# Soft-MoE attention: six of eight batches taken two at a time in logits, dispatch softmax and slot products

## The chip, the cores and the metric

The kernel runs on one core of a Trainium2 chip. The metric is the device time of one execution in microseconds (us), lower is better: the median of three runs before the change is 376.43 us (376.32 to 376.77). Of one further execution there is a profile with a trace of every instruction.

## What is computed

First attention for 8 batches, 12 heads, 448 tokens and head size 64, with a sigmoid in place of a softmax. Its result, 3584 tokens of 768 numbers, goes through a soft mixture of 8 experts with 4 slots each (32 slots):

```python
scores = scale * np.matmul(q, k.transpose(0, 1, 3, 2)) - np.log(S)
attn = 1.0 / (1.0 + np.exp(-scores))
x = np.matmul(attn, v)                # then (8 * 448, 768)
...
logits = x @ phi                      # (3584, 32)
d = np.exp(logits - logits.max(0, keepdims=True))
d /= d.sum(0, keepdims=True) + 1e-09  # dispatch: over all tokens
slot_input = d.T @ x
...
h = np.maximum(slot_input[e] @ w1[e], 0.0)
slot_out[e] = h @ w2[e]
...
c = np.exp(logits - logits.max(1, keepdims=True))
c /= c.sum(1, keepdims=True) + 1e-09  # combine: over the slots
out = c @ slot_out
```

All data are float32. The weights w1 and w2 are 50 MB together, q, k and v 33 MB, the output 11 MB.

## The kernel before, in words

Two heads are a head pair, six pairs a batch, 48 in all. Attention goes through a list `seq` of 168 steps, 21 for a batch. At step i TensorE computes the scores of `seq[i]` (`score`, L205) for a block of 128 keys, ScalarE makes the sigmoid (L213), and TensorE multiplies the block of step i - 2 with v (`weigh`, L246): scores run `LAG` = 2 steps ahead. When a head pair is done, ScalarE copies one half of its result out of PSUM (`evac_a`, L249) and VectorE adds the other (`evac_b`, L253). The result is x, with the 128 rows of a head pair as partitions and 448 tokens as columns: tile x0 holds head pairs 0 to 2, xy pairs 3 to 5 of the batch at hand.

Dispatch softmax and slot inputs are made batch by batch while attention goes on, with a maximum that is carried from batch to batch. Four blocks of 128 tokens (`NBK`) hold a batch, the last half filled. The functions are:

- `turns` (L271): VectorE transposes x in 32 x 32 blocks into y (tokens as partitions; y0 for head pairs 0 to 2, y1, which lies in the tile wpe, for 3 to 5). Each of its three calls a batch puts 16 transposes into the queue `todo`; `work` hands them out step by step, by estimated costs and a table `rate`.
- `logits_job` (L287, L295): 24 matmuls of phi and x. For a float32 matmul the trace has two rows. Phi's 32 slots are the columns of the stationary operand, so four matmuls lie side by side in the array, one for each group of 32 columns (j = 0 to 3): group j takes 32 of every 128 tokens. Groups 0 and 1 get 128 moving columns, groups 2 and 3 get 96.
- `softmax_a`, `softmax_b`, `softmax_c` (L304 to L334): maxima, subtraction, sigmoids on ScalarE, reciprocal, product, transposes and sums on VectorE. The logits stay in `lt` for the combine.
- `slot_job` (L340, L359): 32 matmuls, for 4 token blocks, 2 halves of the head pairs and 4 groups of columns; then one VectorE instruction adds the rescaled old sum.

For batch b with u = 21 (b + 1) + 2, the logits come ahead of step u + 1, the sigmoids in u + 2, `softmax_c` in u + 3 and the slot job at the end of step u + 9 (`SLOT_AT`); `slot_job` first hands out all that is left in `todo`. The last batch has a function of its own (`last_job`). The instructions of an engine run in the order in which the code issues them; an engine that waits holds all that stands behind it.

All weight loads go through SP's queue, in units of 384 KB. 56 units (`N_A`) are loaded during attention, spread over the first 140 steps (`W_STEPS`), into the tiles wa0 to wa13, two into wpe near its end, 12 into space that attention leaves, and the rest in transfers of 1536 KB whenever tiles of the ring come free. Behind attention follow the matmuls with w1 (L126), the combine softmax and its transposes (L575), the matmuls with w2 (L645) and the output (L596, L597).

The functions that the change touches:

Of the kernel before, what the change touches and what calls it, by code (L numbers as in the profile page):

```python
# [23 lines left out]
W_STEPS = 140  # L24
# [29 lines left out]
def soft_moe_attention(ctx: ExitStack, tc: tile.TileContext, qk, v, vl, phi, w, wq, wz, cst, out):  # L54
# [13 lines left out]
    lts = [cpool.tile([P, B // 2, P], F32, name=f"lt{t}") for t in range(2)]  # L68
# [4 lines left out]
    def lt_of(b):  # L73
        return lts[b // 4][:, b % 4, :]
# [56 lines left out]
    with ExitStack() as actx:  # L131
# [133 lines left out]
        def turns(t, k0, n):  # L265
            y = (y0, y1)[t]

            def one(a, g):
# [2 lines left out]
                nc.vector.transpose(  # L271
                    y[32 * g:32 * g + 32, k0:k0 + n, 0:nblk(g), BLK * a:BLK * a + BLK], src)
# [19 lines left out]
        def logits_job(b):  # L292
            lg = ps_sc.tile([P, 2, 512], F32, name="sc")[:, 0, :]
            logits(lg, b, range(NPR))
            nc.vector.tensor_copy(lt_of(b)[0:64, :], lg[0:64, 0:P])  # L295
            nc.vector.tensor_copy(lt_of(b)[64:128, 0:96], lg[64:128, 0:96])
            softmax_a(b)

        def softmax_a(b):
            t1 = small.tile([P, 2, 132], F32, name="t1")  # L300
            zt, ls = t1[:, 0, :], lt_of(b)
            for j in range(4):
                r = slice(32 * j, 32 * j + 32)
                nc.vector.tensor_reduce(out=m1[0:32, j:j + 1], in_=ls[r, 0:BLK * nblk(j)], axis=AX.X, op=ALU.max)  # L304
            if b:
                nc.vector.tensor_copy(m1[0:32, 4:5], mz[0:32, (b - 1) % 2:(b - 1) % 2 + 1])
            nc.vector.tensor_reduce(out=m1[0:32, 5:6], in_=m1[0:32, 0:5 if b else 4], axis=AX.X, op=ALU.max)
            new, old = mz[:, b % 2:b % 2 + 1], mz[:, (b - 1) % 2:(b - 1) % 2 + 1]
            for j in range(4):
                nc.vector.tensor_copy(new[32 * j:32 * j + 32, :], m1[0:32, 5:6])  # L310
            if b:
                nc.vector.tensor_tensor(out=zt[:, P:P + 1], in0=old, in1=new, op=ALU.subtract)
            nc.vector.tensor_scalar(zt[:, 0:P], ls, new, None, op0=ALU.subtract)
            dts[b] = t1

        def softmax_b(b):
            zt, pe = dts[b][:, 0, :], dts[b][:, 1, :]
            n = P if b == 0 else P + 1
            nc.scalar.activation(pe[:, 0:n], zt[:, 0:n], AF.Sigmoid)
            nc.scalar.activation(zt[:, 0:n], zt[:, 0:n], AF.Sigmoid, scale=-1.0)  # L320

        def softmax_c(b):
            zt, pe = dts[b][:, 0, :], dts[b][:, 1, :]
            n = P if b == 0 else P + 1
            nc.vector.reciprocal(zt[:, 0:n], zt[:, 0:n])
            nc.vector.tensor_tensor(out=pe[:, 0:n], in0=pe[:, 0:n], in1=zt[:, 0:n], op=ALU.mult)
            nc.vector.transpose(zt[:, 0:P], pe[:, 0:P])
            if b == 0:
                nc.vector.tensor_reduce(out=mz[:, 2:3], in_=pe[:, 0:P], axis=AX.X, op=ALU.add)
            else:  # L330
                nc.vector.tensor_reduce(out=zb, in_=pe[:, 0:P], axis=AX.X, op=ALU.add)
                nc.vector.scalar_tensor_tensor(
                    out=mz[:, 2:3], in0=mz[:, 2:3], scalar=pe[:, P:P + 1], in1=zb, op0=ALU.mult, op1=ALU.add)
            nc.vector.transpose(lt_of(b), lt_of(b))  # L334

        def slot_mm(sls, zt, b, ts, cs=range(NBK), stop=True):
            for c in cs:
                for t in ts:
                    for a in range(4):
                        nc.tensor.matmul(  # L340
                            sls[t][32 * a:32 * a + 32, :], zt[:, c * BLK:(c + 1) * BLK],
                            y_of(t, b)[:, :, c, BLK * a:BLK * a + BLK], start=(c == 0), stop=stop and c == NBK - 1)
# [102 lines left out]
        for b in range(B):  # L445
            u = b * per_b + LAG
            late[u + 10] = [lambda: turns(0, 0, 3)]
            if b < B - 1:
                late[u + 17] = [lambda: turns(1, 0, 2)]
                late[u + 20] = [lambda: turns(1, 2, 1)]  # L450
        for b in range(B - 1):
            u = (b + 1) * per_b + LAG
# [4 lines left out]
            rate.update({u - 2: 1, u - 1: 1, u: 0, u + 1: 0, u + 2: 1.2, u + 3: 0.6, u + 4: 1.2})
# [10 lines left out]
        for i in range(len(seq) + LAG):  # L468
            for f in early.get(i, ()):
                f()  # L470
            if i < len(seq):
# [80 lines left out]
    def combine_softmax(b):  # L552
        lt = lt_of(b).rearrange("p (j s) -> p j s", j=NBK)
        nc.vector.tensor_reduce(out=cm, in_=lt, axis=AX.X, op=ALU.max)
        nc.vector.tensor_tensor(out=lt, in0=lt, in1=cm.unsqueeze(2).broadcast_to([P, NBK, NSLOT]), op=ALU.subtract)  # L555
# [3 lines left out]
        nc.vector.reciprocal(cz, cz)
        nc.vector.tensor_tensor(out=lt, in0=lt, in1=cz.unsqueeze(2).broadcast_to([P, NBK, NSLOT]), op=ALU.mult)  # L560

    def combine_split(b):
        lt = lt_of(b).rearrange("p (j s) -> p j s", j=NBK)
# [4 lines left out]
        return c4

    def combine_turn(b, c4):  # L570
        pt = ps_t.tile([P, 512], F32, name="pt")
        for c in range(NBK):
            n = P if c < 3 else 64
            c0 = c * P if b % 2 == 0 else (c * P + 64) % 448
            nc.tensor.transpose(  # L575
                out=pt[:, c0:c0 + n], in_=c4[0:n, c].rearrange("p a z s -> p (a z s)").bitcast(F32),
                identity=csb[0:n, 0:n])
        at0 = S * b
        while at0 < S * (b + 1):
# [140 lines left out]
```

## Time and profile before

| what | before |
|---|---|
| median of three runs | 376.43 us |
| span of the profiled execution, first to last instruction | 375.5 us |
| TensorE busy | 354.5 us (94%) |
| VectorE busy | 252.7 us (67%) |
| ScalarE busy | 223.9 us (60%) |
| read and written in HBM | 83.59 and 11.01 MB |

In the rows of a profile PE is TensorE, PEld its weight load, DVE VectorE, ACT ScalarE, POOL GpSimd and SP the engine that issues the DMAs; L340 is line 340 of the kernel. A row of the timeline gives start, duration, engine, line, operation, written and read tile, shape and count of a merged group. A row of the groups gives, behind the bar, busy time, mean ns of one, and idle time before them. A row of a windows table gives the stretch, then for PE, PEld, DVE, ACT and POOL the busy time and the number of instructions, then TensorE's granted clock, the DMA share and GB/s. An engine's busy time says nothing of whether others wait for it; that is read where two engines meet.

### The profile page before, as it was taken

The page shows a single profiled execution, that of the slowest core. Times are in us where ns is not written, and L with a number is a line of the kernel's source. Part 1 is how long each engine was busy: PE and PEld are TensorE (multiplying, and loading weights), DVE is VectorE, ACT ScalarE, POOL GpSimd, SP SyncE. Part 2 cuts the span into 40 slices and gives each one's busy share as a digit, 9 for nine tenths or more (in the row PEclk, how much of TensorE's full clock was granted, in tenths as well). Part 3 has the DMA queues.
Part 4 walks back from the last instruction along what each step waited for, and adds up shares of the span by engine and source line. Part 5 has one row for each costly group of instructions (what it writes and reads, how often), then busy time and mean ns, then how long its engine had stood idle before and what let it go on. Part 6 is the DMA issues. An engine that isn't in the chain of part 4 may idle for free.

```text
span 375.5 us, 10520 instructions
## 1 busy us (share of the span) xinstructions
PE 354.5 (94%) x4374; PEld 160.3 (43%) x4374; DVE 252.7 (67%) x681; ACT 223.9 (60%) x309; POOL 5.5 (1%) x25
## 2 busy tenths in 40 slices
PE   8999999999999999999999999999999996999750
PEld 4333444344444444344444444444456552433530
DVE  0048877885979588869869795889655873223560
ACT  4777676766768676767667676768673122423550
POOL 1000000000000000000000000000000000100000
PEclk9999999999999999999999999999999998999895
DMA  7778575766667675766675765534569999999998
GB/s 234 240 233 263 184 234 184 245 210 229 194 200 224 225 223 181 236 227 215 205 225 180 249 227 177 176 101 125 162 186 370 410 426 425 424 427 404 375 404 291
DMA packets 34927, 95.28 MB, mean 254 GB/s; under 512 B 3648, under 2 KB 17344, under 8 KB 33088
## 3 DMA queue, kind: packets, MB, share of 16 engines
q1 hardware_dynamic: 34880, 94.62, 72.3%
q8 instruction: 34, 0.56, 0.6%
q14 instruction: 13, 0.11, 0.1%
HBM read 83.59 MB, written 11.01 MB: 252 GB/s over the span
## 4 chain that ended last, share of the span: by engine, by line
PE 81%; DMA 8%; DVE 6%; ACT 1%; issue 1%; ACTq 0%; DVEq 0%
PE sc L205 34%; PE av L246 33%; DMA wpe<-in_wz_dram 8%; PE sc L287 3%; PE sc L340 3%; PE av L596 2%; PE av L645 1%; PE pt L596 1%; DVE tmp L546 1%; DVE tmp L545 1%; PE av L221 1%; ACT lt L556 1%; PE av L436 1%; DVE lt L555 1%; DVE sm L557 1%
## 5 line engine op out<-in xcount | busy, mean ns | idle before, releaser
L213 ACT ACTIVATE att<-sc,sm 128x896 f32<-128x896 f32 x167 | 168.3, 1008 | 85.1 <-PE sc L205 82.2
L205 PE MATMUL sc<-qk 64*64 64x448 f32 x1336 | 157.5, 543 | 0.0
L246 PE MATMUL av<-att,v 64*64 64x448 f32 x1128 | 131.2, 536 | 0.0
L205 PEld LDWEIGHTS sc<-qk 64*64 64x64 f32 x1336 | 49.7, 134 | 71.0 <-issue 58.4
L271 DVE STREAM_TRANSPOSE wpe<-xy 32x256 f32<-32x256 f32 (+3 forms) x224 | 76.9, 343 | 3.7
L246 PEld LDWEIGHTS av<-att,v 64*64 64x64 f32 x1128 | 42.8, 133 | 63.4 <-issue 61.6
L271 DVE STREAM_TRANSPOSE y<-x 32x288 f32<-32x288 f32 (+1 forms) x128 | 66.5, 520 | 2.0
L253 DVE TENSOR_TENSOR x<-x,av 128x448 f32<-128x448 f32 x24 | 14.9, 621 | 31.6 <-PE av L246 24.6
L246 PE MATMUL av<-att,vl 64*64 64x448 f32 x188 | 22.3, 536 | 0.0
L253 DVE TENSOR_TENSOR xy<-xy,av 128x448 f32<-128x448 f32 x23 | 14.3, 621 | 9.8 <-ACT xy L249 4.4
L126 PE MATMUL av<-wa,jt 128*32 128x256 f32 x336 | 18.5, 380 | 0.1
L126 PEld LDWEIGHTS av<-wa,jt 128*32 128x32 f32 x336 | 10.7, 110 | 7.2 <-DVE jt L402 0.2
L597 ACT COPY wa<-av 128x384 f32<-128x384 f32 x22 | 10.5, 480 | 5.3 <-PE av L596 4.9
L596 PE MATMUL av<-lt,wb 128*128 128x384 f32 x28 | 13.0, 464 | 0.5 <-DVE lt L631 0.5
L597 DVE COPY wa<-pt 128x384 f32<-128x384 f32 x22 | 11.4, 556 | 2.5 <-PE pt L596 2.3
L249 ACT COPY x<-av 128x448 f32<-128x448 f32 x24 | 12.5, 522 | 0.0
L249 ACT COPY xy<-av 128x448 f32<-128x448 f32 x23 | 12.1, 524 | 0.0
L246 PEld LDWEIGHTS av<-att,vl 64*64 64x64 f32 x188 | 7.3, 133 | 10.8 <-issue 10.8
L645 PE MATMUL av<-wa,jt 128*32 128x384 f32 x112 | 11.7, 517 | 0.0
L359 DVE SCALAR_TENSOR_TENSOR jt<-jt,t,sc 128x192 f32<-128x192 f32 x6 | 2.5, 413 | 13.6 <-PE sc L340 13.6
L645 PE MATMUL av<-wa,hw 128*32 128x384 f32 x112 | 11.5, 511 | 0.1
L596 PE MATMUL pt<-lt,wb 128*128 128x384 f32 x28 | 10.5, 374 | 1.1 <-DVE lt L631 1.1
(131 smaller groups left out, 223.1 us busy)
## 6 DMA issues: line engine op xcount, KB each, us to landing
wa<-in_w_dram SPq DMA_DIRECT2D x56, 384.0 KB, 4.0
wa<-in_wq_dram SPq DMA_DIRECT2D x14, 1536.0 KB, 22.6
qk<-in_qk_dram SPq DMA_DIRECT2D x47, 448.0 KB, 3.7
v<-in_v_dram SPq DMA_DIRECT2D x48, 192.0 KB, 2.6
out_dram<-wa SPq DMA_DIRECT2D x12, 384.0 KB, 6.8
out_dram<-wa SPq DMA_DIRECT2D x5, 768.0 KB, 6.2
wb<-in_w_dram SPq DMA_DIRECT2D x6, 384.0 KB, 4.3
wb<-in_w_dram SPq DMA_DIRECT2D x3, 768.0 KB, 7.5
```

The lines of the kernel that those rows point to most:

```text
L126: nc.tensor.matmul(ph[32 * j:32 * j + 32, 0:256], phi_sb[:, kc, :], utile[("w1", e, j, kc // 3)][:, kc % 3 * 256:(kc % 3 + 1) * 256], star ...
L205: nc.tensor.matmul(sc[h][64 * t:64 * t + 64, 0:S], qkts[pt][r, S + k0:S + k0 + 64], qkts[pt][r, 0:S], start=True, stop=True)
L213: nc.scalar.activation(att[:], tile2[:, :, 0:S], AF.Sigmoid, bias=nbias, scale=QSCALE)
L246: nc.tensor.matmul(o[t][r, 0:S], w, att[row, h, :], start=start, stop=stop)
L249: nc.scalar.copy(x_of(p), avs[p][1][:, 0:S])
L253: nc.vector.tensor_tensor(out=x_of(p), in0=x_of(p), in1=av[0][:, 0:S], op=ALU.add)
L271: nc.vector.transpose(y[32 * g:32 * g + 32, k0:k0 + n, 0:nblk(g), BLK * a:BLK * a + BLK], src)
L287: nc.tensor.matmul(lg[32 * j:32 * j + 32, BLK * c0:BLK * n], phi_sb[:, hp, :], blocks(x_of(b * NPR + hp)[:, c0 * P:], j, n - c0), start=(h ...
L340: nc.tensor.matmul(sls[t][32 * a:32 * a + 32, :], zt[:, c * BLK:(c + 1) * BLK], y_of(t, b)[:, :, c, BLK * a:BLK * a + BLK], start=(c == 0) ...
L596: nc.tensor.matmul(pf[:, 0:HALF], ct_of(m, step), sts[hf], start=True, stop=True)
L597: (nc.scalar.copy, nc.vector.tensor_copy)[n % 2](ov, pf[:, 0:HALF])
L645: nc.tensor.matmul(po[32 * fl:32 * fl + 32, 0:HALF], h[:, k:k + NSLOT], ut, start=(n == 0), stop=(n == 2 * E - 1))
```

## The change

Batches (0, 1), (2, 3) and (4, 5) become pairs, batches 6 and 7 stay single (`GROUPS`). Two batches have 896 tokens, exactly seven blocks of 128 (`NB2`). For a pair there is one logits job, one softmax over 224 columns and one slot job over seven blocks, at the places where the second batch of the pair had its own; the first batch of a pair has none. Since x of the first batch must last until the pair's logits, it lies in two weight tiles' space (`wx`, the tiles wa12 and wa13), as do three further blocks of y for each half (`ye`) and the pair's softmax tile (`t1e`). The eight units of those tiles are loaded behind the third pair; the other 48 are spread over 130 steps. A second batch's tokens start in the middle of block 3, so its transposes go to shifted places, 24 a call in place of 16. The host no longer turns the queries of odd batches round by 64 tokens, and the combine takes a pair as pieces of four and three blocks. The core of the diff:

```diff
-W_STEPS = 140
+W_STEPS = 130
+N_X = 8
+GROUPS = ((0, 1), (2, 3), (4, 5), (6,), (7,))
+NB2 = 2 * NBK - 1
...
+        wx = [wpa.tile([P, 4 * UNIT], F32, name=f"wa{(N_A - N_X) // 4 + n}") for n in range(N_X // 4)]
+        xe = [wx[0][:, t * TR * S:(t + 1) * TR * S].rearrange("p (k s) -> p k s", k=TR) for t in range(2)]
...
-        for y in (y0, y1):
-            nc.gpsimd.memset(y[64:128, :, NBK - 1, :], 0.0)
...
-            for g in range(4):
+            if b % 2 == 0 or b >= B - 2:
+                moves = [(g, g, nblk(g), y) for g in range(4)]
+            else:
+                moves = [(g, g + 2, NBK - 1, ye[t]) for g in range(4)]
+                moves += [(g, g - 2, 1, y[:, :, NBK - 1:NBK, :]) for g in (2, 3)]
+            for mv in moves:
                 for a in range(4):
-                    todo.append((0.0335 * n * nblk(g) + 0.18, lambda a=a, g=g: one(a, g)))
+                    todo.append((0.0335 * n * mv[2] + 0.18, lambda a=a, mv=mv: one(a, *mv)))
...
+                for hp in range(NPR):
+                    xa, xb = x_of(g[0] * NPR + hp), x_of(g[1] * NPR + hp)
+                    for x, c0 in ((xa, (0, 0, 0, 0)), (xb, (4, 4, 3, 3))):
+                        for j in (3, 2, 1, 0):
+                            n = nblk(j) if x is xa else NB2 - c0[j]
+                            nc.tensor.matmul(
+                                lg[32 * j:32 * j + 32, BLK * c0[j]:BLK * (c0[j] + n)], phi_sb[:, hp, :],
+                                blocks(x, j if x is xa else (j + 2) % 4, n),
+                                start=(hp == 0 and x is xa), stop=(hp == NPR - 1 and x is xb))
+                nc.vector.tensor_copy(lt, lg[:, 0:NB2 * NSLOT])
...
-            slot_mm([sl[:, t, :] for t in range(2)], dts[b][:, 0, 0:P], b, (0, 1))
+            slot_mm([sl[:, t, :] for t in range(2)], dts[gi][:, 0, :], gi, (0, 1), range(w // NSLOT))
...
-        for b in range(B - 1):
-            u = (b + 1) * per_b + LAG
+        for gi in range(len(GROUPS) - 1):
+            u = (GROUPS[gi][-1] + 1) * per_b + LAG
...
-            rate.update({u - 2: 1, u - 1: 1, u: 0, u + 1: 0, u + 2: 1.2, u + 3: 0.6, u + 4: 1.2})
+            rate.update({u - 2: 1, u - 1: 1, u: 0, u + 1: 0, u + 2: 1.0, u + 3: 0.4, u + 4: 1.2})
...
-                while state["next"] < min(N_A, (i + 1) * N_A // W_STEPS):
+                while state["next"] < min(N_A - N_X, (i + 1) * (N_A - N_X) // W_STEPS):
+                    load(1)
+                if i > W_STEPS and i % 2 == 1 and state["next"] < N_A:
                     load(1)
```

What this does to the order on VectorE, between the softmax of batch 1 (before) and its slot result: the rows start with the addition that makes x of the next batch's first head pair; t and lt are softmax tiles, xy is x of pairs 3 to 5, wpe their y, and the last row takes the slot result.

```order
L253 TENSOR_TENSOR x_91<-x_91,av_878 128x448
L325 RECIPROCAL t_911<-t_911 128x129
L326 TENSOR_TENSOR t_911<-t_911 128x129
L327 STREAM_TRANSPOSE t_911<-t_911 128x128
L331 TENSOR_REDUCE sm<-t_911 128x1
L332 SCALAR_TENSOR_TENSOR sm<-sm,t_911 128x1
L334 STREAM_TRANSPOSE lt_68<-lt_68 128x128
L271 STREAM_TRANSPOSE wpe<-xy 32x4x32 x8
L271 STREAM_TRANSPOSE wpe<-xy 32x3x32 x3
L253 TENSOR_TENSOR x_91<-x_91,av_965 128x448
L271 STREAM_TRANSPOSE wpe<-xy 32x3x32 x5
L359 SCALAR_TENSOR_TENSOR jt<-jt,t_911,sc 128x192
```

The same place with the change, for batches 2 and 3; wa_85 holds the pair's softmax and the further blocks of y.

```order
L359 RECIPROCAL wa_85<-wa_85 128x225
L360 TENSOR_TENSOR wa_85<-wa_85 128x225
L361 STREAM_TRANSPOSE wa_85<-wa_85 128x224
L365 TENSOR_REDUCE sm<-wa_85 128x1
L366 SCALAR_TENSOR_TENSOR sm<-sm,wa_85 128x1
L368 STREAM_TRANSPOSE lt_68<-lt_68 128x224
L285 STREAM_TRANSPOSE wpe<-xy 32x2x32 x7
L285 STREAM_TRANSPOSE wa_85<-xy 32x3x32 x5
L267 TENSOR_TENSOR wa_84<-wa_84,av_1744 128x448
L285 STREAM_TRANSPOSE wa_85<-xy 32x3x32 x11
L285 STREAM_TRANSPOSE wpe<-xy 32x32 x8
L394 SCALAR_TENSOR_TENSOR jt<-jt,wa_85,sc 128x192
```

Behind the addition for the second head pair stood five transposes, now nineteen; the last eight are the first 64 tokens of the second batch, which go into block 3 of wpe.

On TensorE the slot job before, two rows for each token block (y is y0, wpe is y1):

```order
L340 MATMUL sc<-y_94,t_911 32x96 x4
L340 MATMUL sc<-wpe,t_911 32x96 x4
L340 MATMUL sc<-y_94,t_911 32x96 x4
L340 MATMUL sc<-wpe,t_911 32x96 x4
L340 MATMUL sc<-y_94,t_911 32x96 x4
L340 MATMUL sc<-wpe,t_911 32x96 x4
L340 MATMUL sc<-y_94,t_911 32x96 x4
L340 MATMUL sc<-wpe,t_911 32x96 x4
```

And with the change; wa_85 in the last row holds blocks 4 to 6:

```order
L374 MATMUL sc<-y_96,wa_85 32x96 x4
L374 MATMUL sc<-wpe,wa_85 32x96 x4
L374 MATMUL sc<-y_96,wa_85 32x96 x4
L374 MATMUL sc<-wpe,wa_85 32x96 x4
L374 MATMUL sc<-y_96,wa_85 32x96 x4
L374 MATMUL sc<-wpe,wa_85 32x96 x4
L374 MATMUL sc<-y_96,wa_85 32x96 x4
L374 MATMUL sc<-wpe,wa_85 32x96 x4
L374 MATMUL sc<-wa_85 32x96 x24
```

The eight groups of a batch are followed by six more for the three further blocks; the eighth row, block 3 of wpe, is the one that the eight transposes named above complete.

More of the change, by code (lines that the diff above doesn't have):

```diff
@@ L67, in soft_moe_attention @@
     mz, cm, cz, m1, cw = sm[:, 5:9], sm[:, 9:13], sm[:, 13:17], sm[:, 17:23], sm[:, 24:32]
-    lts = [cpool.tile([P, B // 2, P], F32, name=f"lt{t}") for t in range(2)]
+    lts = [cpool.tile([P, B // 2 * P], F32, name=f"lt{t}") for t in range(2)]
     jt = small.tile([P, 2 * SLN], F32, name="jt")
@@ L71, in soft_moe_attention @@
     phi_sb = jt[:, SLN:2 * SLN].rearrange("p (k s) -> p k s", k=NKC)
-    def lt_of(b):
-        return lts[b // 4][:, b % 4, :]
+    lt_at, ltw = [], [0, 0]
+    for gi, g in enumerate(GROUPS):
+        i, wd = gi // 2 - gi // 4, (NB2 if len(g) == 2 else NBK) * NSLOT
+        lt_at.append(lts[i][:, ltw[i]:ltw[i] + wd])
+        ltw[i] += wd
     nc.vector.memset(acc, 0.0)
@@ L290, in logits, with logits_job @@
                         start=(hp == 0), stop=(hp == NPR - 1 and c1 == NBK))
-        def logits_job(b):
+        def logits_job(gi):
+            g, lt = GROUPS[gi], lt_at[gi]
             lg = ps_sc.tile([P, 2, 512], F32, name="sc")[:, 0, :]
[L294 to L301, printed above, removed]
+            if len(g) == 1:
+                logits(lg, g[0], range(NPR))
+                nc.vector.tensor_copy(lt[0:64, :], lg[0:64, 0:P])
+                nc.vector.tensor_copy(lt[64:128, 0:96], lg[64:128, 0:96])
+            else:
+                for hp in range(NPR):
[8 more added lines that the diff above has]
+                nc.vector.tensor_copy(lt, lg[:, 0:NB2 * NSLOT])
+            softmax_a(gi)
@@ L302, in softmax_a @@
+        def softmax_a(gi):
+            t1 = t1e if len(GROUPS[gi]) == 2 else small.tile([P, 2, 132], F32, name="t1")
+            zt, ls = t1[:, 0, :], lt_at[gi]
+            w = ls.shape[1]
             for j in range(4):
                 r = slice(32 * j, 32 * j + 32)
-                nc.vector.tensor_reduce(out=m1[0:32, j:j + 1], in_=ls[r, 0:BLK * nblk(j)], axis=AX.X, op=ALU.max)
-            if b:
-                nc.vector.tensor_copy(m1[0:32, 4:5], mz[0:32, (b - 1) % 2:(b - 1) % 2 + 1])
@@ L307, in softmax_a @@
-            nc.vector.tensor_reduce(out=m1[0:32, 5:6], in_=m1[0:32, 0:5 if b else 4], axis=AX.X, op=ALU.max)
-            new, old = mz[:, b % 2:b % 2 + 1], mz[:, (b - 1) % 2:(b - 1) % 2 + 1]
+                n = w if len(GROUPS[gi]) == 2 else BLK * nblk(j)
+                nc.vector.tensor_reduce(out=m1[0:32, j:j + 1], in_=ls[r, 0:n], axis=AX.X, op=ALU.max)
+            if gi:
+                nc.vector.tensor_copy(m1[0:32, 4:5], mz[0:32, (gi - 1) % 2:(gi - 1) % 2 + 1])
+            nc.vector.tensor_reduce(out=m1[0:32, 5:6], in_=m1[0:32, 0:5 if gi else 4], axis=AX.X, op=ALU.max)
@@ L309, in softmax_a @@
+            new, old = mz[:, gi % 2:gi % 2 + 1], mz[:, (gi - 1) % 2:(gi - 1) % 2 + 1]
             for j in range(4):
                 nc.vector.tensor_copy(new[32 * j:32 * j + 32, :], m1[0:32, 5:6])
[L311 to L318, printed above, removed]
+            if gi:
+                nc.vector.tensor_tensor(out=zt[:, w:w + 1], in0=old, in1=new, op=ALU.subtract)
@@ L319, in softmax_b, with softmax_c @@
+            nc.vector.tensor_scalar(zt[:, 0:w], ls, new, None, op0=ALU.subtract)
+            dts[gi] = t1
+        def softmax_b(gi):
+            zt, pe = dts[gi][:, 0, :], dts[gi][:, 1, :]
+            n = lt_at[gi].shape[1] + (gi > 0)
             nc.scalar.activation(pe[:, 0:n], zt[:, 0:n], AF.Sigmoid)
             nc.scalar.activation(zt[:, 0:n], zt[:, 0:n], AF.Sigmoid, scale=-1.0)
-        def softmax_c(b):
-            zt, pe = dts[b][:, 0, :], dts[b][:, 1, :]
-            n = P if b == 0 else P + 1
+        def softmax_c(gi):
+            zt, pe = dts[gi][:, 0, :], dts[gi][:, 1, :]
+            w = lt_at[gi].shape[1]
+            n = w + (gi > 0)
@@ L330, in softmax_c @@
             else:
-                nc.vector.tensor_reduce(out=zb, in_=pe[:, 0:P], axis=AX.X, op=ALU.add)
+                nc.vector.tensor_reduce(out=zb, in_=pe[:, 0:w], axis=AX.X, op=ALU.add)
                 nc.vector.scalar_tensor_tensor(
-                    out=mz[:, 2:3], in0=mz[:, 2:3], scalar=pe[:, P:P + 1], in1=zb, op0=ALU.mult, op1=ALU.add)
-            nc.vector.transpose(lt_of(b), lt_of(b))
-        def slot_mm(sls, zt, b, ts, cs=range(NBK), stop=True):
+                    out=mz[:, 2:3], in0=mz[:, 2:3], scalar=pe[:, w:w + 1], in1=zb, op0=ALU.mult, op1=ALU.add)
@@ L337, in slot_mm @@
+            nc.vector.transpose(lt_at[gi], lt_at[gi])
+        def slot_mm(sls, zt, gi, ts, cs=range(NBK), stop=True):
             for c in cs:
@@ L341, in slot_mm @@
                             sls[t][32 * a:32 * a + 32, :], zt[:, c * BLK:(c + 1) * BLK],
-                            y_of(t, b)[:, :, c, BLK * a:BLK * a + BLK], start=(c == 0), stop=stop and c == NBK - 1)
+                            y_of(t, gi, c)[:, :, BLK * a:BLK * a + BLK], start=(c == 0), stop=stop and c == cs[-1])
         def add_old(sl, t):
@@ L562, in combine_split, with combine_softmax @@
-    def combine_split(b):
-        lt = lt_of(b).rearrange("p (j s) -> p j s", j=NBK)
+    pieces = []
+    for gi, g in enumerate(GROUPS):
+        for c0, c1 in ((0, NBK), (NBK, NB2))[:len(g)]:
+            lt = lt_at[gi][:, c0 * NSLOT:c1 * NSLOT].rearrange("p (j s) -> p j s", s=NSLOT)
+            pieces.append((lt, c1 - c0, S * g[0] + c0 * P, (c1 - c0) * P if len(g) == 2 else S))
+    def combine_softmax(n):
+        lt, k = pieces[n][:2]
+        m, z = cm[:, 0:k], cz[:, 0:k]
+        nc.vector.tensor_reduce(out=m, in_=lt, axis=AX.X, op=ALU.max)
+        nc.vector.tensor_tensor(out=lt, in0=lt, in1=m.unsqueeze(2).broadcast_to([P, k, NSLOT]), op=ALU.subtract)
+        nc.scalar.activation(lt, lt, AF.Exp)
+        nc.vector.tensor_reduce(out=z, in_=lt, axis=AX.X, op=ALU.add)
+        nc.vector.tensor_scalar(z, z, 1e-9, None, op0=ALU.add)
+        nc.vector.reciprocal(z, z)
+        nc.vector.tensor_tensor(out=lt, in0=lt, in1=z.unsqueeze(2).broadcast_to([P, k, NSLOT]), op=ALU.mult)
@@ L564, in combine_split @@
+    def combine_split(n):
+        lt, k = pieces[n][:2]
         c4 = sb2.tile([P, NBK, 2, 2, NSLOT], F32R, name="tmp")
-        nc.vector.tensor_copy(c4[:, :, 0, 0, :], lt)
-        nc.vector.tensor_tensor(out=c4[:, :, 0, 1, :], in0=lt, in1=c4[:, :, 0, 0, :].bitcast(F32), op=ALU.subtract)
-        nc.scalar.copy(c4[:, :, 1, :, :], c4[:, :, 0, :, :].bitcast(F32))
+        nc.vector.tensor_copy(c4[:, 0:k, 0, 0, :], lt)
+        nc.vector.tensor_tensor(
+            out=c4[:, 0:k, 0, 1, :], in0=lt, in1=c4[:, 0:k, 0, 0, :].bitcast(F32), op=ALU.subtract)
+        nc.scalar.copy(c4[:, 0:k, 1, :, :], c4[:, 0:k, 0, :, :].bitcast(F32))
@@ L568, in combine_split, with combine_turn @@
         return c4
-    def combine_turn(b, c4):
+    def combine_turn(n, c4):
         pt = ps_t.tile([P, 512], F32, name="pt")
-        for c in range(NBK):
-            n = P if c < 3 else 64
-            c0 = c * P if b % 2 == 0 else (c * P + 64) % 448
+        _, k, t0, nt = pieces[n]
+        for c in range(k):
+            w = min(P, nt - c * P)
             nc.tensor.transpose(
[L576 to L579, printed above, removed]
+                out=pt[:, c * P:c * P + w], in_=c4[0:w, c].rearrange("p a z s -> p (a z s)").bitcast(F32),
+                identity=csb[0:w, 0:w])
+        at0 = t0
+        while at0 < t0 + nt:
```

79 lines of the change are left out of this document (39 added, 40 removed).

## The prediction, made before the result was known

> **What bounds the kernel now.** I read first the page's busy shares and slices, then stages with the windows view.
>
> ```profile
> PE 354.5 (94%) x4374; PEld 160.3 (43%) x4374; DVE 252.7 (67%) x681; ACT 223.9 (60%) x309; POOL 5.5 (1%) x25
> DMA  7778575766667675766675765534569999999998
> ...
> 40.20:75.00 34.80, 34.80 (x456) 15.22 (x456) 27.75 (x73) 24.12 (x30) 0.00 (x0) 1.00 0.66 212
> 75.00:109.80 34.80, 34.80 (x454) 15.22 (x456) 28.25 (x76) 24.11 (x30) 0.00 (x0) 1.00 0.67 220
> ```
>
> The two window rows are one batch each (40.20 and 75.00 are the starts of two logits jobs). In a batch TensorE is busy 34.80 of 34.80 us at full granted clock, so for the first 285 us every us that TensorE saves or waits moves the end of attention. VectorE has 28 us in those 34.8: it has room on average, but the mean doesn't say where. Behind attention the DMA digits stand at 9. The chain of waits and SP's timeline show how the two stages hang together:
>
> ```profile
> 286.98 1.41 PE av L126 x24
> ...
> 318.62 29.02 DMA wpe<-in_wz_dram
> 347.68 0.90 PE av L645 x8
> ...
> 288.45 26.83 SPq L114 DMA_DIRECT2D wa<-in_wq_dram  x14
> ```
>
> The 14 large weight loads begin at 288.45 us, when the first expert matmuls (286.98) free their ring tiles, and the transfers that follow end at 347.64 (318.62 + 29.02), when the last matmuls start at once. So the tail is a fixed length of DMA hung on the end of attention: a shift of that end passes to the end of the run whole, and work saved in the tail's combine (three blocks fewer to transpose) lies under the transfers and counts nothing.
>
> **What TensorE saves.** TensorE's timeline around the logits job of batch 1, then around its slot job:
>
> ```profile
> 74.08 0.93 PE L246 MATMUL av<-att,v 64*64 64x448 f32 x8
> 74.94 0.75 PE L287 MATMUL sc<-x,jt 128*32 128x96 f32 x22
> 75.46 0.25 PE L287 MATMUL sc<-xy,jt 128*32 128x96 f32 x2
> 75.53 0.28 PE L287 MATMUL sc<-x,jt 128*32 128x128 f32 x2
> 76.39 0.98 PE L205 MATMUL sc<-qk 64*64 64x448 f32 x8
> 77.19 0.93 PE L246 MATMUL av<-att,v 64*64 64x448 f32 x8
> 78.70 0.56 PE L246 MATMUL av<-att,v 64*64 64x448 f32 x4
> ...
> 89.22 0.93 PE L246 MATMUL av<-att,v 64*64 64x448 f32 x8
> 90.08 0.37 PE L340 MATMUL sc<-y,t 128*32 128x96 f32 x8
> 90.27 0.35 PE L340 MATMUL sc<-wpe,t 128*32 128x96 f32 x8
> 91.26 0.35 PE L340 MATMUL sc<-wpe,t 128*32 128x96 f32 x8
> 92.34 0.93 PE L246 MATMUL av<-att,vl 64*64 64x448 f32 x8
> ```
>
> From one weigh to the next without a job is 1.51 us (77.19 to 78.70). With the logits job it is 3.11 (74.08 to 77.19), with the slot job 3.12 (89.22 to 92.34), so a job costs 1.60 and 1.61 us. Each slot row is a group of four matmuls that lie side by side in the array (x8, since a float32 matmul goes through in two passes). Six groups take 0.99 us (90.27 to 91.26), 0.165 a group or 1.72 ns a column of the moving operand; eight groups are 1.32, and 0.29 is spent on entering and leaving.
>
> *Slot products*: a pair has 7 blocks by 2 halves, 14 groups, in place of twice 8. 14 x 0.165 + 0.29 = 2.60 against 2 x 1.61 = 3.22: 0.62 us saved.
>
> *Logits*: the number of matmuls stays, but the widths change places. In batch 1 two column groups get 128 columns at every step and two get 96, and the rows at 75.46 and 75.53 show that they don't wait for each other: the narrow ones are at the fourth head pair (tile xy) while the wide ones are still at the third (x). The wide ones, 768 columns or 1.32 us, with 0.28 around them, make the 1.60. In the pair each column group gets 128 from one batch and 96 from the other, 1344 columns in all: 2.31 + 0.28 = 2.59 against 3.20, 0.61 saved. (Were they to step together, 12 steps of 0.22 would make 2.92: 0.28 saved.) I take 0.61, since the rows show the groups apart.
>
> Together a pair saves 1.23 us of TensorE, the three pairs **3.7 us**.
>
> **What it costs on VectorE, and who waits.** VectorE turns x into y by block transposes; slot products read y. Its timeline for batch 1, from the logits to the slots (start, duration of the group, line, count), three rows of ScalarE in the same stretch, and mean durations by shape:
>
> ```profile
> 76.51 0.28 DVE L295 COPY lt<-sc 64x128 f32<-64x128 f32 x1 [0.37 <-PE sc L287]
> 77.11 1.07 DVE L304 TENSOR_REDUCE sm<-lt 32x1 f32<-32x128 f32 x4
> 78.20 0.14 DVE L306 COPY sm<-sm 32x1 f32<-32x1 f32 x1
> 79.60 1.53 DVE L271 STREAM_TRANSPOSE wpe<-xy 32x192 f32<-32x192 f32 x4
> 81.24 0.62 DVE L253 TENSOR_TENSOR x<-x,av 128x448 f32<-128x448 f32 x1
> 81.77 0.96 DVE L325 RECIPROCAL t<-t 128x129 f32<-128x129 f32 x1
> 83.97 3.31 DVE L271 STREAM_TRANSPOSE wpe<-xy 32x128 f32<-32x128 f32 x11
> 87.93 1.47 DVE L271 STREAM_TRANSPOSE wpe<-xy 32x96 f32<-32x96 f32 x5
> ...
> 79.91 0.30 ACT L319 ACTIVATE t<-t 128x129 f32<-128x129 f32 x1
> 80.46 0.52 ACT L249 COPY x<-av 128x448 f32<-128x448 f32 x1
> ...
> L271 DVE STREAM_TRANSPOSE wpe<-xy 32x192 f32<-32x192 f32 x56 | 20.8, 372 | 1.0
> L271 DVE STREAM_TRANSPOSE wpe<-xy 32x128 f32<-32x128 f32 x56 | 16.6, 296 | 0.7
> L271 DVE STREAM_TRANSPOSE wpe<-xy 32x96 f32<-32x96 f32 x56 | 15.2, 271 | 1.1
> L559 DVE RECIPROCAL sm<-sm 128x4 f32<-128x4 f32 x8 | 1.4, 180 | 0.3
> L310 DVE COPY sm<-sm 32x1 f32<-32x1 f32 x28 | 4.0, 144 | 0.5
> ```
>
> This is the stretch that decides. From 76.51 VectorE runs nearly without a break to 89.40 (87.93 + 1.47), 12.89 us, and TensorE enters the slot job at 90.08: **0.68 us to spare**. What the pair puts on VectorE here beyond these 0.68 us, TensorE waits for, less what it has to do ahead of the block that comes last. Per pair, by the order of the changed kernel:
>
> - logits out of PSUM: one copy of 224 columns for two. 0.60 (76.51 to 77.11) becomes some 0.43: -0.17.
> - four maxima over 224 in place of 128 or 96 columns, some 1.03 ns a column: 1.09 to 1.54, +0.45; the subtraction +0.10.
> - reciprocal: (957 - 180) / 125 = 6.2 ns a column (the rows L325 and L559), 96 columns more: +0.60.
> - product, two full-height transposes and one sum, 96 columns more each: +0.40.
> - block transposes in the stretch: 4 + 11 + 5 = 20 in 6.31 us now. Then 34: 2 of 192 columns, 8 of 64, 16 of 96, 8 of 32. The three shapes above fit 172 ns + 1.03 ns a column, about 0.015 passes between two, so 0.387, 0.253, 0.286 and 0.22: 9.13 us, +2.82. The 64 and 32 are outside the rows: bounds are the one-column copy (144 + 13 ns) below and the 96-column transpose above, that is 1.27 us less or 0.8 more. I take the line, since three shapes lie on it.
> - ScalarE: its two sigmoids start 0.38 later and are 0.08 longer each; its copy (80.46) is what VectorE's addition (81.24) needs, and VectorE gets there earlier, having two transposes of 192 and one of 64 for four: a wait of 0 to 0.5, I take 0.35.
>
> Sum: +4.55, so 17.44 us from the copy, which starts 0.12 behind the next score (76.51 against 76.39): the last transpose ends **17.56 us** after that score. TensorE enters the slot job 13.69 after it (76.39 to 90.08, steps unchanged), and the block that the eight 32-column transposes complete is the half wpe of block 3, the eighth group: 13.69 + 7 x 0.165 = **14.85**. TensorE waits 17.56 - 14.85 = 2.71 us there, everything behind it in its queue too. The first pair has no carried maximum (L306, and two small ones): 0.40 less, 2.31. Three pairs: **7.7 us**.
>
> [...]
>
> **Moved loads.** In the list of who waited for whom TensorE has waited for no transfer but the last:
>
> ```profile
> PE av L645 <- DMA wpe<-in_wz_dram: 0.4, 1, 0.4
> ```
>
> Eight weight units (384 KB each) now wait for the third pair on SP's queue; the first two of the last tile stand before a v load there, so a late slot job could hold attention's inputs up. I take nothing: that v load waits for a weigh later than the slot job anyway. Batches 6 and 7 keep their work, and the new shares of transposes by step (rate) only move some of them within one stretch, whose sum stays, since slot_job drains the rest ahead of its matmuls.
>
> **Sum.** -3.7 + 7.7 = +4.0 us. The span goes from 375.5 to 379.5; the median of the runs, 376.43, lies 0.9 over the span, so the time is **380.4 us**.
>
> **Rivals.**
> 1. *The short transposes are cheap* (faster). Place: the 16 of 64 and 32 columns before each slot job. At the one-column price (1.27 less) and with no wait for ScalarE (0.35 less) a pair waits 1.62 us less: 7.7 - 4.9 = 2.8 against 3.7, 0.9 faster, 375.5. It decides from 1.3 us a pair on (4.0 / 3); against it, three shapes lie on one line that starts at 172 ns. Chance 0.10. [...]
> 2. *Half of that* (no change): VectorE 1.1 to 1.5 us a pair shorter than summed, the one-column price alone, say (3 x 1.27 = 3.8 less); 376.6. Chance 0.05.
> 3. *Column groups step together in the pair's logits*, as xa and xb alternate: 0.33 a pair lost, 381.4. The rows at 75.46 speak against it. Chance 0.11.
> 4. *Loads late behind the third pair*: one v load up to 2 us late, 382.4. Chance 0.04.
> 5. The forecast: 0.70.
>
> From these: slower 0.85, same 0.05, faster 0.10 (0.2%, 0.75 us, is about what a measurement of this kernel can tell from no change). Within the forecast the transposes' bounds (1.27 less, 0.8 more a pair) and the wait for ScalarE (0.35 less, 0.15 more) would make 4.9 us down and 2.9 up if all held in all pairs; some 60% of that, 3.0 down and 2.0 up, is likely enough to be held, and covers rivals 3 and 4. The range is 377.4 to 382.4.
>
> **What would show it.** Right: in the profile after, TensorE's waits list the slot line behind VectorE's block transposes three times with 2 to 3 us, a pair's logits job is about 2.6 us, and the 32-column transposes take some 0.2 us. VectorE's own wait before the pair's slot result shrinks to the rest of that job. Wrong: slot groups 0.165 us apart all through (rival 1 or 2), or TensorE waiting for a transfer of qk or v.

## The result, and the profile after

The changed kernel takes **380.41 us** (median of 4 runs, 379.49 to 381.22) against 376.38 (376.10 to 376.77) before, a median of four runs now: ratio 1.011, 95% interval 1.0087 to 1.0132, slower by 4.0 us. The forecast was 380.4 us, the range 377.4 to 382.4.

The profiled execution took 380.11 us, its span is 378.3. The page's busy shares have barely moved, which is the first thing to see: nothing in them tells that more than 7 us of waiting have come in.

```profile
PE 350.6 (93%) x4323; PEld 179.9 (48%) x4323; DVE 253.2 (67%) x687; ACT 221.4 (59%) x302; POOL 4.6 (1%) x23
```

TensorE is busy 3.9 us less (350.6 against 354.5), VectorE 0.5 more. Where the saving went stands in the list of who waited for whom (us in total, times, longest), and the tail's beginning and end stand in the chain of waits:

```profile
PE sc L374 <- DVE wpe L285: 4.8, 3, 1.7
...
PE av L691 <- DMA wpe<-in_wz_dram: 0.4, 1, 0.4
```

```profile
289.48 1.42 PE av L132 x24
...
322.89 27.57 DMA wpe<-in_wz_dram
350.51 0.90 PE av L691 x8
```

The slot products now wait for VectorE's block transposes, three times, once for each pair. TensorE's timeline at the second pair's slot job, from the weigh ahead of it to the weigh behind it:

```profile
156.40 0.93 PE L260 MATMUL av<-att,v 64*64 64x448 f32 x8
157.26 0.37 PE L374 MATMUL sc<-y,wa 128*32 128x96 f32 x8
...
158.27 0.35 PE L374 MATMUL sc<-y,wa 128*32 128x96 f32 x8
160.31 0.98 PE L374 MATMUL sc<-wpe,wa 128*32 128x96 f32 x7 [1.69 <-DVE wpe L285]
...
161.13 0.25 PE L374 MATMUL sc<-wpe,wa 128*32 128x96 f32 x1
...
163.10 0.93 PE L260 MATMUL av<-att,vl 64*64 64x448 f32 x8
```

Seven groups go through 0.17 us apart. The eighth, block 3 of wpe, due at 158.44, starts at 160.31 with those of its four column matmuls that have their transposes, and its last one follows at 161.13. From weigh to weigh it is 6.70 us, 1.51 without a job: the slot job costs 5.19. The list of waits says less (4.8 us for all three), since it counts the engine's idle time up to the first of the four. The gap between two weighs is the safer measure.

VectorE's timeline for the same pair, from the logits to the slot result:

```profile
143.70 0.39 DVE L327 COPY lt<-sc 128x224 f32<-128x224 f32 x1 [0.68 <-PE sc L323]
144.13 1.54 DVE L337 TENSOR_REDUCE sm<-lt 32x1 f32<-32x224 f32 x4
...
147.13 0.76 DVE L285 STREAM_TRANSPOSE wa<-xy 32x192 f32<-32x192 f32 x2
147.90 0.23 DVE L285 STREAM_TRANSPOSE wpe<-xy 32x64 f32<-32x64 f32 x1
148.41 0.62 DVE L267 TENSOR_TENSOR wa<-wa,av 128x448 f32<-128x448 f32 x1 [0.27 <-ACT wa L263]
148.95 1.56 DVE L359 RECIPROCAL wa<-wa 128x225 f32<-128x225 f32 x1
...
152.24 1.75 DVE L285 STREAM_TRANSPOSE wpe<-xy 32x64 f32<-32x64 f32 x7
154.02 1.39 DVE L285 STREAM_TRANSPOSE wa<-xy 32x96 f32<-32x96 f32 x5
155.43 0.62 DVE L267 TENSOR_TENSOR wa<-wa,av 128x448 f32<-128x448 f32 x1
156.06 3.11 DVE L285 STREAM_TRANSPOSE wa<-xy 32x96 f32<-32x96 f32 x11
159.19 1.78 DVE L285 STREAM_TRANSPOSE wpe<-xy 32x32 f32<-32x32 f32 x8
162.41 0.41 DVE L394 SCALAR_TENSOR_TENSOR jt<-jt,wa,sc 128x192 f32<-128x192 f32 x1 [1.44 <-PE sc L374]
```

From 143.70 to 160.97 (159.19 + 1.78) there is no break longer than 0.1 us but one of 0.27, and the last of the four column matmuls starts 0.16 behind that end. The wait ends with the row at 159.19: the eight transposes that complete block 3 stand last.

### The profile page after: what moved, and what is told of

It is laid out like the page before. It is cut to its first block, busy times and chain, and to the rows that moved or that the text cites. A ratio compares the mean times of both kernels' runs of the same rounds, so it can differ in the third digit from the quotient of the medians.

```text
span 378.3 us, 10416 instructions
## 1 busy us (share of the span) xinstructions
PE 350.6 (93%) x4323; PEld 179.9 (48%) x4323; DVE 253.2 (67%) x687; ACT 221.4 (59%) x302; POOL 4.6 (1%) x23
## 4 chain that ended last, share of the span: by engine, by line
PE 69%; DVE 17%; DMA 7%; issue 2%; ACT 2%; ACTq 0%; DVEq 0%
PE sc L219 30%; PE av L260 29%; DMA wpe<-in_wz_dram 7%; DVE wa L285 3%; DVE wa L643 2%; DVE wpe L285 2%; PE sc L374 2%; PE sc L323 2%; PE av L691 2%; DVE wa L359 1%; DVE tmp L584 1%; DVE tmp L583 1%; PE sc L305 1%; PE av L235 1%; PE av L472 1%
## 5 line engine op out<-in xcount | busy, mean ns | idle before, releaser
L260 PE MATMUL av<-att,v 64*64 64x448 f32 x1128 | 138.8, 536 | 0.0
L219 PEld LDWEIGHTS sc<-qk 64*64 64x64 f32 x1336 | 60.8, 133 | 61.7 <-issue 44.0
L260 PEld LDWEIGHTS av<-att,v 64*64 64x64 f32 x1128 | 52.0, 133 | 54.0 <-issue 45.7
L285 DVE STREAM_TRANSPOSE wpe<-wa 32x256 f32<-32x256 f32 (+3 forms) x96 | 33.1, 344 | 1.5
L285 DVE STREAM_TRANSPOSE wa<-xy 32x192 f32<-32x192 f32 (+1 forms) x96 | 30.7, 320 | 1.5
L267 DVE TENSOR_TENSOR wa<-wa,av 128x448 f32<-128x448 f32 x18 | 11.2, 621 | 27.5 <-PE av L260 20.7
L285 DVE STREAM_TRANSPOSE y<-wa 32x384 f32<-32x384 f32 (+1 forms) x48 | 24.9, 520 | 0.8
L285 DVE STREAM_TRANSPOSE y<-x 32x96 f32<-32x96 f32 (+2 forms) x56 | 23.1, 413 | 0.8
L285 DVE STREAM_TRANSPOSE wa<-x 32x288 f32<-32x288 f32 x48 | 22.5, 470 | 0.8
L285 DVE STREAM_TRANSPOSE wpe<-xy 32x64 f32<-32x64 f32 (+5 forms) x80 | 21.6, 270 | 1.4
```

The source lines that it names most:

```text
L219: nc.tensor.matmul(sc[h][64 * t:64 * t + 64, 0:S], qkts[pt][r, S + k0:S + k0 + 64], qkts[pt][r, 0:S], start=True, stop=True)
L260: nc.tensor.matmul(o[t][r, 0:S], w, att[row, h, :], start=start, stop=stop)
L267: nc.vector.tensor_tensor(out=x_of(p), in0=x_of(p), in1=av[0][:, 0:S], op=ALU.add)
L285: nc.vector.transpose(dst[32 * g:32 * g + 32, k0:k0 + n, 0:m, BLK * a:BLK * a + BLK], src)
```

## The experiments

All start from the changed kernel. "Wait" is a pair's slot job less 2.60 us, which it costs in the next run, where it waits for nothing.

**Slot jobs of the pairs two steps later (later).** The theory is that the work is sound and only its due time is wrong. Diff (the second edit keeps the next batch's transposes behind the job, the third the loads):

```diff
-SLOT_AT = 9
+SLOT_AT = 11
...
-            late[u + 10] = [lambda b=b: turns(b, 0, 0, 3)]
+            late[u + (12 if b in (2, 4, 6, 7) else 10)] = [lambda b=b: turns(b, 0, 0, 3)]
...
-                if i > W_STEPS and i % 2 == 1 and state["next"] < N_A:
+                if i > W_STEPS + 2 and i % 2 == 1 and state["next"] < N_A:
```

> The pair's slot job two steps (3.0 us) later, and the next batch's first transposes with it, so that VectorE's work ahead of the slot job stays the same and gets 3.0 us more. Theory (TensorE waits for VectorE's last block transposes): the last transpose ends 17.56 us after the score behind the logits, block 3 is now reached at 14.85 + 3.0 = 17.85, so the three waits of 2.3 to 2.7 us go, a pair's slot job costs 2.6 us as summed, and attention ends some 7.5 us earlier than with the change as it was, 3.7 earlier than before: 372.7 us. Rival (the jobs over a pair are long for another reason, say the wider logits and softmax): nothing of this moves, 380.4 us.

Measured: 373.96 us (373.37 to 374.67), ratio 0.9933 (0.9913 to 0.9953). TensorE at the second pair's slot job:

```profile
158.38 0.93 PE L260 MATMUL av<-att,v 64*64 64x448 f32 x8
159.24 0.37 PE L374 MATMUL sc<-y,wa 128*32 128x96 f32 x8
...
160.42 0.35 PE L374 MATMUL sc<-wpe,wa 128*32 128x96 f32 x8
160.58 1.17 PE L374 MATMUL sc<-wa 128*32 128x96 f32 x48
...
162.49 0.93 PE L260 MATMUL av<-att,v 64*64 64x448 f32 x8
```

The job is 4.11 - 1.51 = 2.60 us in one piece, in all three pairs. So the wait was the whole loss, and without it the change is a gain. It came out 1.3 us over the number of the theory, for the most part because a wait of another kind came in at the end of attention, where batch 7 is moved too and its transposes come late:

```profile
277.43 0.76 PE L305 MATMUL sc<-x,jt 128*32 128x96 f32 x22 [0.75 <-DVE sc L523]
```

That is 0.75 us, and batch 6's logits job is 0.18 longer (3.29 us from weigh to weigh, 244.36 to 247.65, in place of 3.11). In the profile attention, from the first weigh to the first expert matmuls, is 276.42 us, 2.7 shorter than before: about the 3.7 of the theory less these 0.93.

**The memsets put back (memsets).** The profiled execution after is ahead of before by 1.46 us when attention has hardly begun (first weigh at 6.26 against 7.72). The changed kernel no longer clears the unused half of y0 and y1 on GpSimd at the start, so that could be the reason:

```diff
+        for y in (y0, y1):
+            nc.gpsimd.memset(y[64:128, :, NBK - 1, :], 0.0)
```

> The two memsets of y on GpSimd put back at the start. In the profile with the change TensorE was at full clock from 4.4 us on, before from 7.3 us on, and the first scores were done 1.5 us earlier. If the memsets made that difference, the first weigh starts at 7.7 us again and the time is 1.5 us longer, 381.9. If the moment is set by something that varies from run to run whatever the kernel, the time stays within 379.5 to 381.2, and the first weigh may start anywhere from 6.3 to 7.7.

Measured: 380.54 us (380.05 to 381.46), ratio 1.0108 (1.0083 to 1.0134), no different from the change. Its profile's first weigh starts at 7.64. Both theories fit one profile; what decides is that *later* and the kernels below, without the memsets, have theirs at 7.13 to 7.80 (the last of them, *cold*, apart). So the early start belongs to this one execution and not to the edit.

**Block 3 first (order).** The eight transposes that TensorE waits for go ahead of the eight of block 4:

```diff
-                moves = [(g, g + 2, NBK - 1, ye[t]) for g in range(4)]
-                moves += [(g, g - 2, 1, y[:, :, NBK - 1:NBK, :]) for g in (2, 3)]
+                moves = [(g, g - 2, 1, y[:, :, NBK - 1:NBK, :]) for g in (2, 3)]
+                moves += [(g, g + 2, NBK - 1, ye[t]) for g in range(4)]
```

> In the second batch of a pair the transposes that complete block 3 are put ahead of those of blocks 4 to 6; same instructions, same places otherwise. Theory: VectorE ends at the same moment, but what comes last is now needed two groups later (13.69 + 9 x 0.165 = 15.18 in place of 14.85), so each wait is 0.33 us shorter, 1.0 in all: 379.4. Rival (TensorE's wait is for the whole of VectorE's work, not for the last block): no difference, 380.4.

Measured: 380.34 us (379.83 to 380.44), ratio 1.0097 (1.0074 to 1.0120): no different. TensorE's and VectorE's timelines at the second pair:

```profile
157.25 0.93 PE L260 MATMUL av<-att,v 64*64 64x448 f32 x8
158.11 0.37 PE L374 MATMUL sc<-y,wa 128*32 128x96 f32 x8
...
161.20 1.92 PE L374 MATMUL sc<-wa 128*32 128x96 f32 x40 [1.40 <-DVE wa L285]
...
163.86 0.93 PE L260 MATMUL av<-att,vl 64*64 64x448 f32 x8
```

```profile
147.97 1.14 DVE L285 STREAM_TRANSPOSE wa<-xy 32x192 f32<-32x192 f32 x3
...
153.09 1.92 DVE L285 STREAM_TRANSPOSE wa<-xy 32x192 f32<-32x192 f32 x5
155.03 1.55 DVE L285 STREAM_TRANSPOSE wpe<-xy 32x32 f32<-32x32 f32 x7
...
157.49 4.57 DVE L285 STREAM_TRANSPOSE wa<-xy 32x96 f32<-32x96 f32 x16
```

The expectation's mechanism happened: nine rows now go through, and the wait has moved from the eighth row to the tenth. But the job went from 5.19 to 6.61 - 1.51 = 5.10, 0.09 less in place of 0.33, because VectorE ended at 162.06, 3.95 us behind TensorE's entry (158.11), where it had been 160.97 - 157.26 = 3.71. The rows show where the 0.24 comes from. The edit turns the order round in every call of `turns` for a second batch, in the earlier call for pairs 3 and 4 too. Of that call, eight transposes of 192 columns are now left for the stretch between logits and slot job (1.14 + 1.92 us), where with the change it was two of 192 and eight of 64 (0.76 + 0.23 + 1.75 us): 0.3 more, most of which stays. So "VectorE ends at the same moment" was the step that failed. The time alone can't tell the expectation from its rival, as the interval holds both 379.4 and 380.4; the place of the wait can, and it speaks against the rival.

**Half the transposes (merged).** The second batch's x of pairs 3 to 5 is turned in one go instead of pairs 3, 4 and pair 5 apart: 24 block transposes fewer a pair, same columns.

```diff
-                late[u + 17] = [lambda b=b: turns(b, 1, 0, 2)]
-                late[u + 20] = [lambda b=b: turns(b, 1, 2, 1)]
+                if b % 2 == 0:
+                    late[u + 17] = [lambda b=b: turns(b, 1, 0, 2)]
+                late[u + 20] = [lambda b=b: turns(b, 1, *((2, 1) if b % 2 == 0 else (0, 3)))]
```

> In the second batch of a pair the two calls of turns for head pairs 3 to 5 become one, ahead of the last batch step: 24 transposes of up to 288 columns in place of 48. The fixed share of 24 transposes (172 ns and 15 between two, 4.5 us) goes, but the work starts three steps later. Theory (a fixed price of some 0.19 us an instruction): up to 20 us for what lay between the end of the batch and the slot job become some 18, so the waits shrink from 2.3 to 2.7 to about 1.5 us each, 3 us in all: 377.4. Rival (short transposes are priced by their columns): nothing is saved and the later start makes the waits longer, over 381.

Measured: 378.17 us (376.92 to 379.01), ratio 1.0042 (1.0026 to 1.0058). VectorE's last rows and TensorE's wait at the second pair:

```profile
156.83 1.44 DVE L285 STREAM_TRANSPOSE wa<-xy 32x288 f32<-32x288 f32 x3
158.29 2.32 DVE L285 STREAM_TRANSPOSE wpe<-xy 32x96 f32<-32x96 f32 x8
```

```profile
156.79 0.93 PE L260 MATMUL av<-att,v 64*64 64x448 f32 x8
...
159.75 1.18 PE L374 MATMUL sc<-wpe,wa 128*32 128x96 f32 x7 [0.74 <-DVE wpe L285]
...
162.74 0.93 PE L260 MATMUL av<-att,vl 64*64 64x448 f32 x8
```

The slot jobs are 3.99, 4.44 and 4.45, waits of 1.4, 1.8 and 1.8 in place of 2.3, 2.6 and 2.6. With the same columns and fewer instructions the wait shrinks by 0.8 to 0.9 us, 2.4 in all where the theory had 3, and the time by 2.2. The rival wanted longer waits and is out: the count of instructions on VectorE ahead of the slot job moves the time. The fixed part of a short transpose is most of its price (by the prediction's line 172 of the 204 ns that 32 columns take).

**One step later (ten).** If the wait is VectorE's lateness and nothing else, a slot job one step (1.5 us) later must wait that much less, neither nothing nor as much:

```diff
+SLOT_PAIR = 10
...
-            late[u + 10] = [lambda b=b: turns(b, 0, 0, 3)]
+            late[u + {2: 11, 4: 11, 6: 11, 7: 10}.get(b, 10)] = [lambda b=b: turns(b, 0, 0, 3)]
...
-            late[u + SLOT_AT] = [lambda gi=gi: slot_job(gi)]
+            late[u + (SLOT_PAIR if gi < 3 else SLOT_AT)] = [lambda gi=gi: slot_job(gi)]
...
-                if i > W_STEPS and i % 2 == 1 and state["next"] < N_A:
+                if i > W_STEPS + 2 and i % 2 == 1 and state["next"] < N_A:
```

> A dose between the change and the run called later: the pairs' slot jobs one step (1.50 us) later, the single slot job and batch 7 as with the change. Theory: with the change the three pairs' slot jobs cost 2.31, 2.59 and 2.59 us more than in the run called later, where nothing waits; one step takes 1.5 off each, so 0.8, 1.1 and 1.1 stay, a slot job of a pair is 3.4 to 3.7 us long, and the time is 4.5 us below the change: 375.9. Rival (the run called later gained by something that switches, not by time given to VectorE): the waits are all there or all gone, 380.4 or 373.

Measured: 375.83 us (374.90 to 377.28), ratio 0.9982 (0.9968 to 0.9997). TensorE at the second pair:

```profile
157.06 0.93 PE L261 MATMUL av<-att,vl 64*64 64x448 f32 x8
...
159.48 0.98 PE L375 MATMUL sc<-wpe,wa 128*32 128x96 f32 x7 [0.19 <-DVE wpe L286]
...
162.26 0.93 PE L261 MATMUL av<-att,v 64*64 64x448 f32 x8
```

5.20 - 1.51 = 3.69: the wait is 1.09, 1.50 less than the 2.59 of the change, one step. At nine, ten and eleven steps the ratios are 1.011, 0.998 and 0.991 (the last from *later9*, below): the price of the wait as a function of the due time, with the next batch's transposes and the last weight loads moved along.

**Two steps later for the pairs only (later9).** Batches 6 and 7 stay where they were, which should take away the wait at the end that *later* brought:

```diff
+SLOT_PAIR = 11
...
-            late[u + 10] = [lambda b=b: turns(b, 0, 0, 3)]
+            late[u + {2: 12, 4: 12, 6: 12, 7: 10}.get(b, 10)] = [lambda b=b: turns(b, 0, 0, 3)]
...
-            late[u + SLOT_AT] = [lambda gi=gi: slot_job(gi)]
+            late[u + (SLOT_PAIR if gi < 3 else SLOT_AT)] = [lambda gi=gi: slot_job(gi)]
...
-                if i > W_STEPS and i % 2 == 1 and state["next"] < N_A:
+                if i > W_STEPS + 2 and i % 2 == 1 and state["next"] < N_A:
```

> As the run called later for the three pairs, but batch 6's slot job and batch 7's transposes stand where the change has them (steps 9 and 10). In the run called later TensorE waited 0.75 us for VectorE's memset at the end of attention and 0.18 in the last logits job. Theory: batch 7's transposes, two steps late, made both, and batch 6 alone has room (its last transpose ended 2.5 us ahead of its slot job, which now comes 3.0 earlier, block 3 another 1.15 behind): attention 0.7 to 0.9 us shorter than in the run called later, 373.2. Rival: batch 6's slot job now waits and takes it back, 374.0 or more.

Measured: **373.68 us** (372.14 to 373.89), ratio 0.9913 (0.9894 to 0.9932), the fastest median of all. The logits job that waited in *later* (now at L306) enters without a wait:

```profile
276.77 0.75 PE L306 MATMUL sc<-x,jt 128*32 128x96 f32 x22
```

From the first weigh to the first expert matmuls it is 275.92 us, 0.5 shorter than *later*, where the theory had 0.7 to 0.9. The 0.75 is gained; 0.31 is given back in batch 6's slot job (262.97 - 259.54 = 3.43 from weigh to weigh, in place of 3.12), whose transposes now have less time, so that part of the rival came true. And batch 6's logits job is still 0.18 longer (3.29): batch 7's late transposes, which the theory blames for both waits of *later*, don't make that one. The medians differ by 0.28, which the intervals don't separate; the gaps in the two profiles do.

**No warm-up (cold).** With *later9*, the five matmuls on zeros at the start left out (nothing is computed from them), to see whether they set the moment at which TensorE comes to its full pace:

```diff
-WARM = 5
+WARM = 0
```

> The run called later9 without the five warm-up matmuls that TensorE does on zeros from 1.1 to 3.6 us, ahead of the first scores; nothing is computed from them. In the profiles so far the first scores ran at half pace until 4.4 to 7.4 us after the start, 3.3 to 6.3 behind TensorE's first matmul. Theory: the full clock is granted some time after TensorE became busy, within one to two stretches of 3.4 us; without the warm-up the same delay starts 2.5 us later, at 3.6, so the slow part of the scores is about 2.5 us longer, half of which is lost: about 1.2 us slower, 374.9. Rival (the clock comes a fixed or random time after the start, whatever TensorE does): no difference, 373.7.

The stretch of 3.4 us stands in before's record of the clock: its entries last 307.20 us at full speed, 3.41 at half, 34.13 at full, 3.41 at half and 10.24 at full, ahead of the last one, all whole multiples of 3.41.

Measured: 374.05 us (373.16 to 374.60), ratio 0.9931 (0.9913 to 0.9950), 0.37 above *later9* with intervals that overlap. Its first weigh starts at 8.08, the latest of nine profiles, but only 0.3 behind the latest with a warm-up (7.80). Full speed begins at 7.96 in its trace, 4.3 us behind TensorE's first matmul (3.67); in the eight others it is 3.3 to 6.2 behind that (1.12), so both theories can live with it. This settles nothing.

## Why the prediction was right, point by point

**What bounds the kernel.** The tail is a fixed length hung on the end of attention: from the first expert matmuls to the last weight transfer it is 60.79 us before (286.89 to 347.68) and 61.12 after (289.40 to 350.51). Fixed holds to about 1 us: in the nine profiles it is 59.6 to 61.4, so these 0.3 us say nothing of the change. The combine's saved transposes don't show in it, as forecast.

**Savings.** The pair's logits job, again from weigh to weigh, at the second pair:

```profile
140.27 0.93 PE L260 MATMUL av<-att,v 64*64 64x448 f32 x8
141.13 0.43 PE L323 MATMUL sc<-wa,jt 128*32 128x96 f32 x8
141.32 0.40 PE L323 MATMUL sc<-x,jt 128*32 128x128 f32 x8
141.54 0.40 PE L323 MATMUL sc<-wa,jt 128*32 128x96 f32 x8
...
144.37 0.93 PE L260 MATMUL av<-att,v 64*64 64x448 f32 x8
```

4.10 - 1.51 = 2.59, as forecast. The rows come 0.19 and 0.22 apart, then 0.16 and 0.22 in turn (0.19 on average) and not 0.22 throughout, so the column groups don't step together and rival 3 is out. The slot job is 2.60 where it doesn't wait, as forecast. A pair saves some 1.23 us, three pairs 3.7, as forecast.

**The wait.** Slot jobs of 4.92, 5.19 and 5.20 us in place of 2.60 are waits of **2.32, 2.59 and 2.60, 7.5 us**, against 2.31, 2.71, 2.71 and 7.7. The steps behind it, at the second pair: VectorE's stretch is 17.27 us (17.44), its end 17.40 behind the score (160.97 - 143.57; 17.56), TensorE's entry 13.69 behind it (157.26 - 143.57, as forecast), and block 3 is the place. The wait for ScalarE is 0.27 in the profile (0.35). The terms by which it was most uncertain are these rows (by shape; behind the bar us in total, mean ns, and idle time before):

```profile
L285 DVE STREAM_TRANSPOSE wpe<-xy 32x64 f32<-32x64 f32 x24 | 5.7, 238 | 0.3
L285 DVE STREAM_TRANSPOSE wpe<-xy 32x32 f32<-32x32 f32 x24 | 4.9, 204 | 0.5
```

The line of 172 ns + 1.03 ns a column gives 238 and 205. Rivals 1 and 2 needed these to be cheap, and fall with them; *merged* says the same from the other side.

**Loads.** TensorE waits for no transfer of qk or v in the list of waits; rival 4 did not happen.

**The sum.** 7.5 - 3.7 = +3.8 us from the jobs. Attention, from the first weigh to the first expert matmuls, is 4.0 us longer (283.14 against 279.16). The other 0.2 shows at the first pair's logits job, which takes 4.31 us from weigh to weigh in this profile and 4.09 in the seven others with pairs; it belongs to the one execution. In *memsets*, whose jobs are the same, attention is 282.93, 3.8 longer than before.

**What was wrong.** Two readings of the span, neither of them part of the mechanism. "The median of the runs, 376.43, lies 0.9 over the span" put together numbers of different executions. Every run that was timed here lies 1.8 us (1.73 to 1.86) above its own span, so the profiled execution of before, with its 375.5, took some 377.3 and was 0.9 slower than the median. The forecast of the time does not suffer, since to add 4.0 to the span and then 0.9 is to add 4.0 to the median. And the span after is 378.3, not 379.5, since that one execution began 1.5 us earlier (below): the span's +2.8 are 4.0 in attention, 0.3 in the tail, and 1.5 off at the start. A comparison of the two spans alone would have read the loss nearly a third too small.

## What to carry to other kernels

A mean of 67% busy says nothing about the stretch ahead of a consumer: count what is queued on the slower engine between the last input and the last thing that the consumer needs, and compare it with when the consumer enters; here 0.7 us of slack, and 1.2 more until the eighth row, met 4.4 us of new work (17.27 us in place of 12.89). When merging two units of work saves time on the bounding engine but makes the side engine's block longer, move the consumer's due time by as much before judging the merge: the same change was 4.0 us slower at step 9 and, by the medians, 2.7 faster at step 11. Many short block transposes are dearer than the same columns in few: one of 192 columns and one of 96 took 370 and 270 ns with the change, one of 288 took 470 in *merged*.

## What the runs showed of the hardware

When TensorE comes to its full pace is not the same in every execution. The first score rows and the first weigh in before and in after:

```profile
3.63 3.27 PE L205 MATMUL sc<-qk 64*64 64x448 f32 x16
6.67 1.22 PE L205 MATMUL av<-qk 64*64 64x448 f32 x8
7.72 0.92 PE L246 MATMUL av<-att,v 64*64 64x448 f32 x8
```

```profile
3.55 2.13 PE L219 MATMUL sc<-qk 64*64 64x448 f32 x16
5.51 0.92 PE L219 MATMUL av<-qk 64*64 64x448 f32 x8
6.26 0.92 PE L260 MATMUL av<-att,v 64*64 64x448 f32 x8
```

The same 16 rows take 3.27 us in one and 2.13 in the other, without a wait. In the traces' records of the clock the first entry at full speed begins at 7.26 us in before and at 4.40 in after, and between 5.91 and 7.96 in the seven others (the windows view has 1.00 from the start and doesn't show it). Until then the matmuls go at half the pace: in before the next rows start 3.04 us after the first 16 (3.63 to 6.67), where later a step of 16 such rows takes 1.51. So about half of such a difference is lost: up to 1.5 us between two profiles of kernels that start alike (first weigh at 6.26 and 7.80). The spans of the timed runs of one kernel differ by as much and more (373.4 to 375.8 in before, 377.7 to 379.4 after), which fits, but their starts aren't in any trace. Neither the memsets nor, as far as one profile tells, the warm-up moves it beyond this spread; what sets it stays open. For reading profiles it means: compare stages by their own length, and starts apart.
